# Scores as 64x64 tiles, two units in one train: a change to a fused attention and bilinear kernel on Trainium2

## The chip, the cores and the metric

The kernel runs on one core of one Trainium2 chip. The metric is the device time in microseconds (us), from one launch to its end; lower is better. "A unit" below is a block of 128 positions of one batch element, all eight heads. There are 4 x 6 = 24 of them.

## What is computed

A decaying linear attention in blocks, and behind it a bilinear feed-forward layer:

```
B, H, S, D = 4, 8, 768, 64
Dmask   = where(i >= j, lam ** (i - j), 0)              # inside a block
intra   = ((q_b @ k_b.T) * Dmask) @ v_b                 # scores, then attention output
inter   = (q_b * lam ** (i + 1)) @ kv_state             # what came before the block
out_b   = intra + inter
kv_state = lam ** block * kv_state + (k_b * lam ** (block - 1 - i)).T @ v_b

x = out.transpose(0, 2, 1, 3).reshape(B * S, H * D)     # 3072 x 512
y = ((x @ w_a) * (x @ w_b)) @ w_out                     # d_ff = 1536
```

The kernel takes blocks of 128 positions and puts the decay into scaled q and k.

## The kernel before

The 24 units are worked through in groups of 4, 2, 4, 4, 4, 4, 2. While TensorE does the feed-forward layer of one group, the attention of later units is put in between at "slots", by a plan. From group 1 on the products of the feed-forward layer are made with seven partial products in place of eight (`m_q`, `m_r`, `m_p` for the first two matrices, `o_q`, `o_p`, `o_r` for the last one); the additions this takes fall to VectorE and GpSimd.

The plan for groups 2, 3 and 4 ends with these steps; `_u` is 10, 14 and 18:

```python
for _g, _u in ((2, 10), (3, 14), (4, 18)):
    PLAN[_g] += [(11, "V", _u), (13, "Q", (_u, _u + 1, _u + 2)), (14, "V", _u + 2), (14, "S", _u + 3),
                 (16, "SK", _u + 4), (16, "OD", (_u + 2, _u + 3)), (17, "SM", _u + 4)]
```

V updates the state of a unit, S makes scores and masks them, SK makes scores and holds their banks, SM masks what SK left, Q makes the attention output of two units with the scores of a third, OD makes the output of two units.

PSUM has seven banks that rotate (an eighth holds the state). A bank is given out by longest-unused among those that are not held; reading a tile out, or releasing it, marks it as just used:

```python
    def ps_bank(name, shape, dt, hold=False, at=None):
        i = at
        if i is None:
            i = min((i for i in range(7) if i not in bank["held"]), key=lambda i: bank["age"][i])
        touch(i)
        if hold:
            bank["held"].add(i)
        ...
```

Scores, the products with the state (`inter`) and the attention products (`intra`). Where an operand or a result takes only 64 of the 128 partitions, the matmul uses only that half of the array's rows or columns:

```python
    def scores(u, kq=None):
        d = U[u]
        kq = kq or score_banks()                 # two banks, kq0 and kq1
        for hp in range(HP):                     # HP = 4 pairs of heads
            for i in range(2):
                p = slice(64 * i, 64 * i + 64)
                nc.tensor.matmul(kq[i][:, hp, :], lhsT=d["kT"][p, hp, :], rhs=d["qT"][p, hp, :],
                                 start=True, stop=True, skip_group_check=True)
        return kq

    def o_mm(u, b, c, **ops):
        h = 4 * b + c
        p = slice(64 * (h % 2), 64 * (h % 2) + 64)
        ...
        nc.tensor.matmul(U[u]["o"][b][p, c // 2, :], start=new[b, h % 2], stop=True, ...)

    def inter(u):
        if u % NB > 0:                           # NB = 6 units of a batch element
            st = st_bufs[(u - 1) % 4]
            for c in range(HP):
                for b in range(2):
                    p = slice(64 * b, 64 * b + 64)
                    o_mm(u, b, c, lhsT=st[p, c, b, :], rhs=U[u]["qT"][p, c, :])

    def intra(u, b):
        for c in range(HP):
            o_mm(u, b, c, lhsT=vbs[u][:, 4 * b + c, :], rhs=U[u]["m"](b, c))

    def pieces_O(us, nxt=(), defer=False):       # "Q": us = two units, nxt = the third
        kqs = [score_banks() for u in nxt]
        o_banks(us)                              # two banks o_ps for both units
        for u, kq in zip(nxt, kqs):
            scores(u, kq)
        for u in us:
            inter(u)
        for b in range(2):
            for u in us:
                intra(u, b)
            evac_o(us, b)                        # ScalarE copies o_ps[b] to xT, marks the bank
        ...
        if beside:
            kv_beside(us[1])                     # state products, 128x64
        ...                                      # masks of nxt, on VectorE; mark kq0, kq1

    def piece_SK(u):
        kq = U[u]["kq"] = scores(u)
        return kq.ids                            # the plan holds these two banks

    def piece_SM(u):
        kq = U[u].pop("kq")
        masks(u, kq)
        return kq.ids                            # the plan lets them go
```

The last matrix of groups 2 to 4, up to where o_r is taken (FC is 12):

```python
        q, qb = bank_of("o_q")                   # held
        product(q, of_x(0, 0), of_w(0, 0), js, True)
        s1 = snap("o_s1", "c12", q, 2)
        ...
            p, pb = bank_of("o_p")
            product(p, of_x(0, 1), of_w(1, 0), js[:2], True)
            xs4 = [blocks(j) for j in js]
            add_sums(js[:2], (0, 1))
            last_step()                          # last m_q product; VectorE: ab = c22 * m_q; m_q's bank released
            hook(FC)
            product(p, of_x(0, 1), of_w(1, 0), js[2:], False)
        o1, o2 = out_tile(), out_tile()
        nc.vector.tensor_add(o1[:, :, 0:256], s1, p)
        release(pb)                              # o_p's bank
        if not early:
            add_sums(js[2:], (0, 1))
        hook(FC + 1)                             # slot 13
        r, rb = bank_of("o_r")
        product(r, of_s(0), of_t(0), js, True)
        s5 = snap("o_s5", "s5", r, 2)
        if not early:
            hook(FC + 2)                         # slot 14
        ...
        product(q, of_s(1), of_t(1), js, False)
        u2 = snap("o_u2", "c12", q, 2)
        ...
        hook(FC + 3)
        hook(FC + 4)                             # slot 16
        product(q, of_s(2), of_t(2), js, False)
```

Of the kernel before, what the change touches and what calls it, by code (L numbers as in the profile page):

```python
# [61 lines left out]
    5: [(6, "SA", 23), (8, "SB", 23), (11, "V", 22), (13, "O2", (22, 23))],  # L62
}
for _g, _u in ((2, 10), (3, 14), (4, 18)):
    PLAN[_g] += [(11, "V", _u), (13, "Q", (_u, _u + 1, _u + 2)), (14, "V", _u + 2), (14, "S", _u + 3),
                 (16, "SK", _u + 4), (16, "OD", (_u + 2, _u + 3)), (17, "SM", _u + 4)]
PLAN[2] += [(_s, "W", None) for _s in (3, 3, 3, 4, 4, 4)]

# [2 lines left out]
def kernel(  # L71
# [11 lines left out]
    nc = tc.nc  # L83
    B, H, S, D = q.shape
# [244 lines left out]
    def score_banks():  # L329
        kq = Banks()  # L330
        kq.ids = []
        for i in range(2):
            kq.append(ps_bank(f"kq{i}", [128, HP, 128], F32))
            kq.ids.append(bank["last"])
# [4 lines that stand above are left out]
        kq = kq or score_banks()  # L339
        for hp in range(HP):  # L340
            for i in range(2):
                p = slice(64 * i, 64 * i + 64)
                nc.tensor.matmul(kq[i][:, hp, :], lhsT=d["kT"][p, hp, :], rhs=d["qT"][p, hp, :],  # L343
                                 start=True, stop=True, skip_group_check=True)
        return kq

    def masks(u, kq):
# [98 lines left out]
    def piece_S(u):  # L446
        masks(u, scores(u))

    def piece_SA(u):
        kq = U[u]["kq"] = scores(u)  # L450
        U[u]["ms"] = [mask_one(kq, 0)]
        return [kq.ids[1]]

    def piece_SK(u):
        kq = U[u]["kq"] = scores(u)
        return kq.ids
# [644 lines left out]
```

## Time and profile before

| what | value |
|---|---|
| time, median of 3 runs | 216.6 us (216.32 to 216.92) |
| span of the profiled execution | 214.6 us |
| TensorE clock granted | 1.00 |
| PE time by the chain, line 594 (m_q, m_r, m_p) | 25%, 13% and 6% |
| PE time by the chain, scores (kq, line 343) | 3% |
| score matmuls of units 4 to 23 (line 343) | 160, of 64 rows x 128 columns |
| state products into o_ps from these units (line 379) | 136 records, 64x64 |
| attention products into o_ps (line 379) | 192, of 128 rows x 64 columns |
| DMA, mean | 146 GB/s |

PE is TensorE's matmuls and PEld its weight loads; DVE is VectorE, ACT ScalarE, POOL GpSimd. A shape such as 64*128 behind a matmul is the part of the array used: rows by columns. A matmul's length in the profile runs to its modelled end and overlaps its neighbours', so the pace is read from one start to the next. Slots have no name in the profile; they are found by the order of tensors on PE.

### The profile page before, as it was taken

The numbers are of one execution on the slowest core, as the hardware profiler recorded it, in microseconds if no ns is written. First come the engines' busy times: TensorE is split into PE (matmuls) and PEld (weight loads), VectorE is DVE, ScalarE is ACT, GpSimd is POOL, SyncE is SP. The second block draws the span as 40 slices with busy tenths as digits, with TensorE's granted clock in tenths as the row PEclk, the third lists the DMA queues.
The fourth block names the chain that finished last, engine by engine and source line by source line (L and its number), as shares of the span: only waits on it lengthen the run. The fifth ranks groups of instructions, "written<-read, shape, count | busy, mean of one in ns | idle before, by whom it ended". The sixth has DMA issues, their size and how long they took to land.

```text
span 214.6 us, 5764 instructions
## 1 busy us (share of the span) xinstructions
PE 208.5 (97%) x2323; PEld 162.6 (76%) x2331; DVE 176.9 (82%) x322; ACT 106.8 (50%) x195; POOL 124.2 (58%) x143
## 2 busy tenths in 40 slices
PE   7899999999999999999999999999999999999994
PEld 2476444555995788878888988888988888889973
DVE  0892899987897997998989998989998788896860
ACT  3686224156852556436555534555444656343621
POOL 5879669983769299810699610799700846400320
PEclk9999999999999999999999999999999999999999
DMA  4999999999999999992299990399900480002202
GB/s 126 303 180 189 201 231 216 239 219 185 128 203 165 163 181 267 245 187 44 105 164 209 261 148 3 111 179 170 233 0 3 120 152 0 3 2 92 107 3 98
DMA packets 86766, 31.31 MB, mean 146 GB/s; under 512 B 74068, under 2 KB 83156, under 8 KB 86740
## 3 DMA queue, kind: packets, MB, share of 16 engines
q1 hardware_dynamic: 53748, 20.39, 48.0%
q0 software_dynamic: 32704, 10.49, 42.7%
q8 instruction: 18, 0.29, 0.6%
q10 hardware_dynamic: 288, 0.07, 0.1%
q14 instruction: 8, 0.07, 0.1%
HBM read 28.32 MB, written 6.29 MB: 161 GB/s over the span
## 4 chain that ended last, share of the span: by engine, by line
PE 93%; DMA 3%; SPq 1%; issue 0%; ACT 0%; DVE 0%
PE m_q L594 25%; PE m_r L594 13%; PE op L832 10%; PE o_q L705 9%; PE m_p L594 6%; PE o_r L705 5%; PE o_ps L379 5%; PE b_ps L517 5%; PE a_ps L517 5%; PE kq L343 3%; DMA k<-in_k_dram 3%; PE o_p L705 2%; PE kvd L410 2%; SPq L229 1%; PE tps L321 1%; PE o_w L705 1%
## 5 line engine op out<-in xcount | busy, mean ns | idle before, releaser
L594 PEld LDWEIGHTS <-tw 128*128 128x128 bf16 x576 | 48.7, 98 | 5.4
L641 POOL TENSOR_TENSOR ab<-c,c 128x512 bf16<-128x512 bf16 x30 | 34.9, 1170 | 28.2 <-DVE c L639 27.8
L594 PE MATMUL m_q<-xs,tw 128*128 128x256 bf16 (+1 forms) x288 | 36.1, 255 | 0.0
L594 PEld LDWEIGHTS <-wa_sb 128*128 128x128 bf16 x288 | 24.7, 98 | 2.6
L609 ACT COPY s<-m_q 128x512 f32<-128x512 f32 x30 | 17.7, 589 | 17.2 <-PE m_q L594 17.1
L648 DVE TENSOR_TENSOR ab<-c,m_q 128x512 bf16<-128x512 f32 x30 | 20.5, 684 | 5.9 <-PE m_q L594 4.0
L360 DVE TENSOR_TENSOR m<-kq,lotri 128x512 bf16<-128x512 f32 x39 | 24.6, 681 | 0.7 <-PE kq L343 0.7
L298 POOL DMA_DIRECT2D vb<-in_v_dram x24 | 22.4, 935 | 1.4 <-DMA wo_sb<-in_moe_w_out_dram 1.2
L832 PE MATMUL op<-wo_sb,ab 128*128 128x512 bf16 (+2 forms) x114 | 22.1, 335 | 0.4 <-issue 0.2
L639 DVE TENSOR_TENSOR c<-u,m_r 128x512 f32<-128x512 f32 x30 | 20.4, 681 | 2.3 <-ACT u L609 2.3
L609 ACT COPY s<-m_r 128x512 f32<-128x512 f32 x30 | 17.7, 590 | 9.0 <-PE m_r L594 9.0
L609 ACT COPY u<-m_q 128x512 f32<-128x512 f32 x30 | 17.7, 591 | 6.9 <-PE m_q L594 5.7
L645 DVE TENSOR_TENSOR c<-s,m_q 128x512 f32<-128x512 f32 x30 | 20.6, 686 | 0.6
L628 DVE TENSOR_TENSOR c<-s,m_p 128x512 bf16<-128x512 f32 x25 | 17.1, 686 | 3.9 <-PE m_p L594 3.6
L1039 POOL COPY gate<-xs 1x1 bf16<-1x1 bf16 x3 | 0.5, 178 | 34.3 <-DVE xs L575 34.3
L705 PEld LDWEIGHTS <-sm 128*128 128x128 bf16 x192 | 17.9, 98 | 2.9 <-DVE sm L738 0.2
L276 POOL TENSOR_TENSOR qk<-qf,lp_q 128x512 bf16<-128x512 f32 x18 | 18.9, 1048 | 0.0
L402 ACT CAST xT<-o_ps 128x512 bf16<-128x512 f32 x22 | 11.9, 589 | 13.4 <-PE o_ps L379 13.2
L594 PE MATMUL m_r<-xs,tw 128*128 128x256 bf16 (+1 forms) x144 | 18.1, 255 | 0.0
L594 PE MATMUL m_q<-xT,tw 128*128 128x256 bf16 (+1 forms) x144 | 18.1, 255 | 0.0
L594 PE MATMUL m_r<-xs,wb_sb 128*128 128x256 bf16 (+1 forms) x144 | 18.1, 255 | 0.0
L594 PE MATMUL m_p<-xT,wa_sb 128*128 128x256 bf16 (+1 forms) x144 | 18.1, 255 | 0.0
(120 smaller groups left out, 382.7 us busy)
## 6 DMA issues: line engine op xcount, KB each, us to landing
out_dram<-o_two SPq DMA_DIRECT2D x8, 512.0 KB, 3.2
qf<-in_q_dram SPq DMA_DIRECT2D x14, 256.0 KB, 5.4
kf<-in_k_dram SPq DMA_DIRECT2D x14, 256.0 KB, 5.8
vb<-in_v_dram POOLq DMA_DIRECT2D x24, 128.0 KB, 5.6
wa_sb<-in_moe_w_a_dram POOLq DMA_DIRECT2D x6, 256.0 KB, 6.2
wb_sb<-in_moe_w_b_dram POOLq DMA_DIRECT2D x6, 256.0 KB, 7.6
wo_sb<-in_moe_w_out_dram POOLq DMA_DIRECT2D x6, 256.0 KB, 8.1
out_dram<-o_kept SPq DMA_DIRECT2D x6, 256.0 KB, 5.1
```

Source lines behind the costliest of these rows:

```text
L276: eng_of(eng).tensor_mul(dst.rearrange("p (c b) d -> p b c d", b=2), x[:].rearrange("p (b c) d -> p b c d", b=2), lp.rearrange("p (b c) o ...
L298: nc.gpsimd.dma_start(out=vb, in_=vr[b, nb])
L360: nc.vector.tensor_mul(m, kq[i], lotri_bc)
L517: nc.tensor.matmul(ps[:, lo:hi], lhsT=w_sb[:, s, f * 128:(f + 1) * 128], rhs=xT[:, s, lo:hi], start=(s == 0), stop=(s == KS - 1), skip_gro ...
L594: nc.tensor.matmul(ps[:, f, :], lhsT=w(k, f), rhs=x[:, k, :], start=(first and f == 0 and k == 0), stop=True, skip_group_check=True)
L609: nc.scalar.copy(t, ps)
L639: nc.vector.tensor_add(c12, d["u2"], d["r"])
L641: nc.gpsimd.tensor_mul(ab[:, nf * i:nf * i + nf, 0:h], d["c11"], c12)
L645: nc.vector.tensor_add(d["c22"], d["s5"], d["q"])
L648: nc.vector.tensor_mul(ab[:, nf * i:nf * i + nf, h:2 * h], d["c22"], d["q"])
L705: nc.tensor.matmul(ps[:, t, :], lhsT=x(j, c)[:, t * BLK:(t + 1) * BLK], rhs=w(j)[:, c, :], start=(first and t == 0 and j == js[0] and c == ...
L832: nc.tensor.matmul(op[:, lo:hi], lhsT=ab[:, f, t * 128:(t + 1) * 128], rhs=wo_sb[:, f, lo:hi], start=(f == 0), stop=(f == FC - 1))
```

## The change

The scores of a unit are cut along the columns too: 16 matmuls of 64x64 in place of 8 of 64x128, the same shape that the state products have. Between a train of scores and the state products behind it TensorE then keeps its shape. In groups 2 to 4 the scores of unit `_u + 3` leave slot 14 and go ahead of those of unit `_u + 2` at slot 13, in one train with them, with their two banks held until slot 14, where VectorE masks them as before. Both parts are meant to spare TensorE changes of shape. On VectorE, ScalarE, GpSimd and the queues the order of instructions stays as it was; the banks that the tiles get are others.

```diff
 for _g, _u in ((2, 10), (3, 14), (4, 18)):
-    PLAN[_g] += [(11, "V", _u), (13, "Q", (_u, _u + 1, _u + 2)), (14, "V", _u + 2), (14, "S", _u + 3),
+    PLAN[_g] += [(11, "V", _u), (13, "SK", _u + 3), (13, "Q", (_u, _u + 1, _u + 2)), (14, "V", _u + 2), (14, "SM", _u + 3),
                  (16, "SK", _u + 4), (16, "OD", (_u + 2, _u + 3)), (17, "SM", _u + 4)]

@@ scores
         for hp in range(HP):
             for i in range(2):
                 p = slice(64 * i, 64 * i + 64)
-                nc.tensor.matmul(kq[i][:, hp, :], lhsT=d["kT"][p, hp, :], rhs=d["qT"][p, hp, :],
-                                 start=True, stop=True, skip_group_check=True)
+                for c in (0, 64):
+                    nc.tensor.matmul(kq[i][c:c + 64, hp, :], lhsT=d["kT"][p, hp, c:c + 64], rhs=d["qT"][p, hp, :],
+                                     start=True, stop=True, skip_group_check=True)
         return kq
```

## The prediction

> **What bounds the kernel now.** I read the page's table of engines first, then the chain that ended last. Columns of the first: busy time, share of the span, instructions.
>
> ```profile
> PE 208.5 (97%) x2323; PEld 162.6 (76%) x2331; DVE 176.9 (82%) x322; ACT 106.8 (50%) x195; POOL 124.2 (58%) x143
> ...
> PE 93%; DMA 3%; SPq 1%; issue 0%; ACT 0%; DVE 0%
> ```
>
> TensorE works from end to end, and the chain names no other engine after the first inputs have landed. The list of waits has only a few tenths of a microsecond for PE after the start. So every nanosecond put on or taken off the PE queue counts in full, and whatever makes PE wait is new time. Busy time does not show the tile mode, though: matmuls overlap, and a switch of mode hides inside a "busy" stretch. For that I read the time line of PE alone (start, length, engine, line, tensors, count), here at slot 13 of group 2:
>
> ```profile
> 93.32 0.60 PE L705 MATMUL o_p<-wo_sb,ab 128*128 128x256 bf16 x4
> 93.86 0.40 PE L343 MATMUL kq<-qkT 64*128 64x128 bf16 x8
> 94.18 0.42 PE L379 MATMUL o_ps<-qkT,st 64*64 64x128 bf16 x16
> 94.53 0.64 PE L379 MATMUL o_ps<-m,vb 128*64 128x128 bf16 x16
> 95.10 0.61 PE L705 MATMUL o_r<-two,sm 128*128 128x256 bf16 x4
> ```
>
> and from slot 14 to the end of slot 16:
>
> ```profile
> 96.56 0.39 PE L410 MATMUL kvd<-vb,qk 128*128 128x128 bf16 x4
> 96.88 0.40 PE L343 MATMUL kq<-qkT 64*128 64x128 bf16 x8
> 97.21 1.48 PE L705 MATMUL o_q<-two,sm 128*128 128x256 bf16 x12
> 98.63 0.40 PE L343 MATMUL kq<-qkT 64*128 64x128 bf16 x8
> 98.95 0.31 PE L379 MATMUL o_ps<-qkT,st 64*64 64x128 bf16 x8
> 99.19 0.64 PE L379 MATMUL o_ps<-m,vb 128*64 128x128 bf16 x16
> ```
>
> Read the differences of starts. Full-array matmuls of 256 columns follow each other every 0.109 us, so the four o_p should hand over at 93.32 + 0.44 = 93.76; the scores start at 93.86. That 0.10 us is the switch 128x128 to 64x128. A score train lasts 0.327 us from its first start to the next mode's first start (the single starts in the trace: 93.855 and 94.183). A train of 16 state products lasts 0.347 (94.183 to 94.530), one of 8 lasts 0.236 (98.952 to 99.188): 8 more cost 0.111, so four square tiles go through together every 0.056 us. The scores in pairs also have 0.056 us per pair.
>
> **What the Trainium skill says.** "TensorEngine Tiling (Array Packing)", Key Properties: changing the tiling mode drains TensorE, and different tiles load and multiply in parallel. The trace agrees with both: 0.09 to 0.10 us more at every change of shape, four square tiles per 0.056 us. The same page, Restrictions and Gotchas, says that column tiling switches off the fast weight load. The trace shows loads of 103 to 110 ns for 64 columns against 92 to 96 for the scores' 128, but the state products keep their 0.056 all the same, so I charge nothing for it. "PSUM — Partial Sum Buffer", Terms (PSUM bank): TensorE and a reader may not be on one bank at once. So a bank has to be read out before it is written again; no run here shows a collision, only waits.
>
> **The change part by part.**
> Square tiles. A unit's 8 score matmuls of 64x128 become 16 of 64x64: four rounds of four tiles in place of four pairs, at the same 0.056 us. Where full-array work stands on both sides the new train should look like the 16 state products: 0.347 against 0.327, +0.02 us. There are 160/8 = 20 trains. Ten stand alone (units 4 to 7, 9, 10, 11, 15, 19, 23): +0.20 us.
> Where state products come next there is no switch any more: 8 rounds in one mode cost 0.347 + 4 x 0.056 = 0.57 against 0.327 + 0.347 = 0.67, so -0.10 us. That is four trains without counting slot 13: unit 8 in group 1 and units 14, 18, 22 at slot 16: -0.41 us.
> The moved train. At slot 14 kvd's four matmuls should take 4 x 0.056 = 0.22 us, yet o_q starts 0.65 us after them. Without unit 13's scores there, 0.43 to 0.44 us go (the first matmul behind a switch is also 0.01 late). Three groups: -1.31 us. At slot 13 the four more rounds cost 0.22 us, less 0.10 for the switch saved: +0.12 each, +0.37 in all.
> Without new waits this sums to 0.20 - 0.41 - 1.31 + 0.37 = -1.15 us, 215.4 us. That is what the change is after.
>
> **Banks.** Slot 13 is where I think this fails. The seven rotating PSUM banks go out by longest-unused. o_q holds one. Before, the slot asks for two score banks and two for o_ps, and six are free: the two most recent, those of the last m_q and of o_p, stay untouched. Then o_r takes m_q's. Changed, the two banks of unit u+3 are held as well: 1 + 2 + 2 + 2 = 7. The two o_ps, asked for last, get exactly m_q's and o_p's banks. Both are still being read by VectorE:
>
> ```profile
> 94.01 0.68 DVE L648 TENSOR_TENSOR ab<-c,m_q 128x512 bf16<-128x512 f32 x1
> 94.61 0.68 DVE L771 TENSOR_TENSOR o_two<-o_s,o_p 128x512 f32<-128x512 f32 x1
> ```
>
> The order of instructions of the changed kernel has a wait for VectorE on the first matmul into each o_ps, which confirms it. VectorE works without a gap there, in an unchanged order, so it cannot come sooner. The first state product goes into m_q's bank; the second goes into o_p's and can start at 94.608 + 0.678 + 0.055 = 95.34 (0.055: after the sums of L738 end at 95.620, o_r goes on at 95.677). Two units' scores end at about 93.86 + 0.08 + 7 x 0.056 = 94.33, so PE stands for 1.0 us. Compared with 94.19 before, the second state product is 1.15 late.
>
> Then o_r. Four unheld banks are left, and the longest unused is o_ps's first, marked when ScalarE copies it out; the score banks are marked later, with the masks. The changed order has a ScalarE wait on the first o_r. The copy:
>
> ```profile
> 94.99 1.07 ACT L402 CAST xT<-o_ps 128x512 bf16<-128x512 f32 x2 [2.13 <-PE o_ps L379]
> ```
>
> The first of the two starts 0.456 after the attention products do (94.986 - 94.530) and takes 0.586; with 0.055 for the release, o_r may start 1.10 us after the attention products. Before, it starts 0.57 after them. That is 0.53 us more, of which 0.13 was spent later anyway on o_r's wait for its sums (four o_r from 95.10 end at 95.54, the fifth starts at 95.677).
> Group 2: 1.15 + 0.53 - 0.13 = +1.55 at the end of o_r; -0.44 for the moved train, -0.10 at slot 16: **+1.01 us**.
> Groups 3 and 4 have the same banks; VectorE is earlier in proportion:
>
> ```profile
> 125.93 0.42 PE L379 MATMUL o_ps<-qkT,st 64*64 64x128 bf16 x16
> ...
> 125.89 0.67 DVE L771 TENSOR_TENSOR o_two<-o_s,o_p 128x512 f32<-128x512 f32 x1
> ...
> 157.65 0.31 PE L379 MATMUL o_ps<-qkT,st 64*64 64x128 bf16 x8
> ...
> 157.61 0.67 DVE L771 TENSOR_TENSOR o_two<-o_s,o_p 128x512 f32<-128x512 f32 x1
> ```
>
> In group 3 the second state product can start at 125.887 + 0.674 + 0.055 = 126.62 against 125.93: +0.68. There eight kvd products lie between the attention products and o_r (0.69 instead of 0.57), so o_r waits 0.40 more. 0.68 + 0.40 - 0.44 - 0.10 = **+0.54**. Group 4: 157.612 + 0.729 = 158.34 against 157.65, the same sum: **+0.55**. These already contain the scores' 0.22, hidden in the stall.
> Sum: 1.01 + 0.54 + 0.55 + 0.20 (trains alone) - 0.10 (unit 8) = **+2.2 us**. 216.6 becomes 218.8; I take 218.7, as VectorE may catch up a little while PE stands.
>
> **Rivals.** (1) The gain comes as meant: 215.4. For it: each switch's 0.10 us is real and PE is the only bound. Against it: two named waits, on banks whose readers end after PE wants them. (2) Only the first wait bites, because the copies out of o_ps come sooner or o_r finds its bank free: 0.53 - 0.13 + 0.40 + 0.40 = 1.2 less, 217.6. Against it: ScalarE cannot start before the attention products it copies. (3) Square tiles are slower than state products, through 16 loads where 8 were, say 0.1 us a train: 20 x 0.1 = 2 more, 220.8. Against it: the state products, with the same shapes, show 0.056 per four. (4) Unit u+3's transposed q and k come too late at slot 13, some 3 us sooner than before. Against it: unit 13's transpose is issued at 82.1, 17's at 115.1, 21's at 148.7, and landing takes at most 7.5 us.
>
> **Range and chances.** The stalls are differences of measured ends and depend on one engine's fixed order; I give each 0.3 us. 217.5 to 219.7 holds most of it, down to rival 2 and up to half of rival 3. The 2% bounds are 212.3 and 220.9: faster would need over 4 us from switches that cost 0.1 each; slower needs rival 3 in full. Faster 0.01, within 0.96, slower 0.03.
>
> **What would show it.** PE's list of waits after the start should hold o_ps waiting for L771 three times (about 1.0, 0.5, 0.5 us as the trace sees idleness, less what running matmuls cover), and o_r for the copy of L402 three times, each about 0.4 to 0.5. Score trains next to state products without the 0.09 gap would show the first part right; score rounds slower than 0.056, or 0.35 us exceeded by a lone train, would show it wrong. If o_ps starts at once behind the scores, my reading of the banks is wrong, and the time goes to 215.4.

## The result, and the profile after

The changed kernel takes 218.68 us (median of 5 runs, 218.56 to 218.92) against 216.73 of the kernel before: 1.0088 times as long, 95% interval 1.0068 to 1.0109. It is slower by about 1.9 us (1.5 to 2.4 by the interval), inside the predicted 217.5 to 219.7. The profiled span is 217.1 against 214.6.

The page and the list of what TensorE (PE) waited for, in the changed kernel (engine, line, tensor, then the releaser; us in total, times, longest):

```profile
PE 207.9 (96%) x2491; PEld 163.1 (75%) x2491; DVE 176.1 (81%) x322; ACT 106.8 (49%) x195; POOL 124.7 (57%) x143
...
PE 85%; DVE 6%; DMA 3%; issue 1%; SPq 1%; ACT 1%
...
PE o_r L706 <- ACT xT L403: 1.1, 3, 0.5
PE o_ps L380 <- DVE o_two L772: 1.0, 3, 0.4
```

The kernel before had neither wait. PE falls from 93% to 85% of the chain that ended last, and VectorE (DVE) comes in with 6%: the chain now runs through the readers of PSUM banks, and from them back along VectorE's own work, so the 6% (13 us) are more than the stalls. On the time line of PE, slot 13 of group 2 (start, length, engine, line, tensors, count, idle time before and its releaser):

```profile
93.68 0.60 PE L706 MATMUL o_p<-wo_sb,ab 128*128 128x256 bf16 x4
94.21 0.64 PE L344 MATMUL kq<-qkT 64*64 64x128 bf16 x32
95.08 0.21 PE L380 MATMUL o_ps<-qkT,st 64*64 64x128 bf16 x1 [0.23 <-DVE ab L649]
95.68 0.41 PE L380 MATMUL o_ps<-qkT,st 64*64 64x128 bf16 x15 [0.39 <-DVE o_two L772]
96.02 0.64 PE L380 MATMUL o_ps<-m,vb 128*64 128x128 bf16 x16
97.12 1.47 PE L706 MATMUL o_r<-two,sm 128*128 128x256 bf16 x12 [0.46 <-ACT xT L403]
```

One state product starts, the other fifteen come 0.60 us later, and o_r stands once more. The idle times in brackets are shorter than the stalls, because a matmul's recorded length runs on after the next could have started: the starts say more. On VectorE and ScalarE (ACT) at the same place:

```profile
94.35 0.68 DVE L649 TENSOR_TENSOR ab<-c,m_q 128x512 bf16<-128x512 f32 x1
94.95 0.68 DVE L772 TENSOR_TENSOR o_two<-o_s,o_p 128x512 f32<-128x512 f32 x1
...
96.48 1.07 ACT L403 CAST xT<-o_ps 128x512 bf16<-128x512 f32 x2 [3.27 <-PE o_ps L380]
```

L649 ends at 95.03, and the first product starts at 95.08; L772 ends at 95.63, the others start at 95.68; the first copy ends at 97.07 and o_r starts at 97.12. Each time about 0.05 us after the end of the bank's reader.

Two measures serve for every run below, both in us and from the starts on PE in its profiled execution. The time from the first score of slot 13 to the first score of slot 16 holds nearly everything that the moved train touches. "Whole PE" is the time from the first score of group 0 to the last matmul. Neither has the noise of a launch (the first two profiles differ by 0.24 us before group 0's scores alone).

| kernel | group 2 | group 3 | group 4 | whole PE | device time against before, 95% interval |
|---|---|---|---|---|---|
| before | 4.771 | 4.755 | 4.643 | 200.31 | 1 |
| changed | 5.839 | 5.392 | 5.274 | 202.50 | 1.0088 (1.0068 to 1.0109) |
| e1, square tiles only | 4.780 | 4.667 | 4.557 | 200.00 | 0.9973 (0.9959 to 0.9987) |
| e2, moved train only | 5.867 | 5.386 | 5.277 | 202.68 | 1.0099 (1.0076 to 1.0123) |
| e3, square tiles beside state products only | 4.783 | 4.648 | 4.547 | 200.01 | 0.9976 (0.9960 to 0.9992) |
| e4, banks swapped | 6.062 | 5.606 | 5.496 | 203.17 | 1.0116 (1.0086 to 1.0147) |
| e5, copy in two halves | 5.910 | 5.451 | 5.340 | 202.70 | 1.0082 (1.0059 to 1.0105) |
| e6, o_p copied by ScalarE | 5.249 | 5.116 | 5.005 | 201.38 | 1.0032 (1.0018 to 1.0046) |
| e7, two banks fewer | 4.322 | 4.435 | 4.324 | 199.08 | 0.9933 (0.9917 to 0.9949) |
| e8, banks freed sooner | 4.608 | 4.730 | 4.618 | 199.95 | 0.9970 (0.9955 to 0.9986) |
| e9, as e3 | 4.770 | 4.647 | 4.541 | 199.85 | 0.9985 (0.9969 to 1.0001) |

### The profile page after: what moved, and what is told of

Its sections match the earlier page's. It is cut to its first block, busy times and chain, and to the rows that moved or that the text cites. A ratio compares the mean times of both kernels' runs of the same rounds, so it can differ in the third digit from the quotient of the medians.

```text
span 217.1 us, 6092 instructions
## 1 busy us (share of the span) xinstructions
PE 207.9 (96%) x2491; PEld 163.1 (75%) x2491; DVE 176.1 (81%) x322; ACT 106.8 (49%) x195; POOL 124.7 (57%) x143
## 4 chain that ended last, share of the span: by engine, by line
PE 85%; DVE 6%; DMA 3%; issue 1%; SPq 1%; ACT 1%
PE m_q L595 23%; PE m_r L595 12%; PE op L833 10%; PE o_q L706 7%; PE m_p L595 6%; PE o_r L706 5%; PE a_ps L518 5%; PE b_ps L518 5%; PE o_ps L380 5%; DMA k<-in_k_dram 3%; PE kq L344 2%; DVE sm L739 1%; SPq L229 1%; PE kvd L411 1%; DVE ab L649 1%
## 5 line engine op out<-in xcount | busy, mean ns | idle before, releaser
L649 DVE TENSOR_TENSOR ab<-c,m_q 128x512 bf16<-128x512 f32 x30 | 20.6, 685 | 5.9 <-PE m_q L595 4.0
L833 PE MATMUL op<-wo_sb,ab 128*128 128x512 bf16 (+2 forms) x120 | 23.1, 337 | 0.0
L595 PE MATMUL m_q<-xT,wa_sb 128*128 128x256 bf16 (+1 forms) x144 | 18.1, 255 | 0.0
```

Source lines behind the costliest of these rows:

```text
L595: nc.tensor.matmul(ps[:, f, :], lhsT=w(k, f), rhs=x[:, k, :], start=(first and f == 0 and k == 0), stop=True, skip_group_check=True)
L649: nc.vector.tensor_mul(ab[:, nf * i:nf * i + nf, h:2 * h], d["c22"], d["q"])
L833: nc.tensor.matmul(op[:, lo:hi], lhsT=ab[:, f, t * 128:(t + 1) * 128], rhs=wo_sb[:, f, lo:hi], start=(f == 0), stop=(f == FC - 1))
```

## The experiments

The theory: the two-unit train takes the last two free PSUM banks while VectorE still reads them, and o_r then has to take one that ScalarE still reads. The rivals: square tiles are slow; or the state products and o_r wait for something of their own.

### The two parts apart

**e1**, the plan of before and square tiles everywhere; **e2**, the other way round:

```diff
 # e1: before.py with
+                for c in (0, 64):
+                    nc.tensor.matmul(kq[i][c:c + 64, hp, :], lhsT=d["kT"][p, hp, c:c + 64], rhs=d["qT"][p, hp, :], ...)
 # e2: before.py with
+    (13, "SK", _u + 3), (13, "Q", (_u, _u + 1, _u + 2)), (14, "V", _u + 2), (14, "SM", _u + 3),
```

> Square score tiles with the plan of before. My theory (a switch of mode costs about 0.10 us, four square tiles go every 0.056 us, a lone square train costs 0.02 us more): 7 trains next to state products save 0.10 each, 13 lone ones lose 0.02 each, -0.46 us, 216.2 against 216.7 of before, no wait of PE on o_ps or o_r. Rival (square tiles are slower through 16 weight loads where 8 were, and this is what cost the 2 us): 217.5 or more.

> The two-unit train at slot 13 with the scores still 64x128. My theory (both stalls come from the two banks held more): the stalls are set by the end of VectorE's and ScalarE's reads, so they stay; groups 2 to 4 lose 1.11, 0.64 and 0.65, 219.1 us. Rival (the moved train by itself saves, and the loss comes from the square tiles): below 216.7.

e1 took 216.23 us against 216.69 of before, 0.9973 times; e2 took 218.78, 1.0099 times. The moved train alone costs what the whole change costs, and square tiles alone save a little. e2's median lies 0.3 us under the expected 219.1; on PE it is 2.37 us longer than before, where 2.40 was expected. In e2 the waits are those of the changed kernel:

```profile
93.90 0.62 PE L343 MATMUL kq<-qkT 64*128 64x128 bf16 x16
94.80 0.21 PE L379 MATMUL o_ps<-qkT,st 64*64 64x128 bf16 x1 [0.28 <-DVE ab L648]
95.40 0.41 PE L379 MATMUL o_ps<-qkT,st 64*64 64x128 bf16 x15 [0.39 <-DVE o_two L771]
95.74 0.64 PE L379 MATMUL o_ps<-m,vb 128*64 128x128 bf16 x16
96.83 0.38 PE L705 MATMUL o_r<-two,sm 128*128 128x256 bf16 x2 [0.46 <-ACT xT L402]
```

At slot 13 it makes no difference which shape the scores have: the switch that square tiles save is hidden in the stall.

e1's median came out as expected (-0.46), but that is luck: its interval is -0.9 to -0.3, and from the first score of group 0 to the last matmul it saves 0.31. Each of the seven trains beside state products was to save 0.10. In groups 3 and 4 and at slot 16 of group 2 they do: 0.248 us from the first score to the first state product in place of 0.327, and 0.024 more inside the state products. Two give nothing. In group 1, behind unit 8's scores, the state products of before and of e1, with VectorE's read of m_p:

```profile
61.18 0.69 DVE L628 TENSOR_TENSOR c<-s,m_p 128x512 bf16<-128x512 f32 x1 [0.28 <-PE m_p L594]
...
61.45 0.40 PE L343 MATMUL kq<-qkT 64*128 64x128 bf16 x8
...
61.78 0.45 PE L379 MATMUL o_ps<-qkT,st 64*64 64x128 bf16 x8
...
62.16 0.64 PE L379 MATMUL o_ps<-m,vb 128*64 128x128 bf16 x16
```

```profile
61.34 0.69 DVE L629 TENSOR_TENSOR c<-s,m_p 128x512 bf16<-128x512 f32 x1 [0.28 <-PE m_p L595]
...
61.60 0.42 PE L344 MATMUL kq<-qkT 64*64 64x128 bf16 x16
...
61.85 0.53 PE L380 MATMUL o_ps<-qkT,st 64*64 64x128 bf16 x8
...
62.31 0.64 PE L380 MATMUL o_ps<-m,vb 128*64 128x128 bf16 x16
```

From the first score to the attention products it is 0.70 us in both: the eight state products contain a pause that was 0.144 us before and is 0.224 now. VectorE's read of m_p ended last there already. It ends at 61.871 before and at 62.021 in e1; the second state product, the first into the other o_ps bank, starts at 61.924 and at 62.076, each time 0.05 us later, as at slot 13 of the changed kernel. The saved switch only lengthens that wait. That this o_ps has m_p's bank is inferred from these times; no run varied it. The second is slot 13 of group 2, where o_r waits for its third sum from VectorE: 1.62 us for its twelve matmuls before, 1.72 in e1. So five trains save 0.10, not seven, and 13 x 0.02 comes off again. Counted from the matmul ahead of a train to the one behind it, a train beside state products saves 0.106 and a lone one costs 0.018, so the terms make 5 x -0.106 + 13 x 0.018 = -0.30, which is what the profile shows (200.00 against 200.31).

**e3** makes only the trains that have state products behind them square, and **e9** is the same kernel once more:

```diff
+BESIDE_STATE = (8, 12, 14, 16, 18, 20, 22)
...
+                if u in BESIDE_STATE:
+                    # two 64x64 matmuls, as in the change
+                    continue
```

> Plan of before; square tiles only in the seven trains that have state products behind them (units 8, 12, 14, 16, 18, 20, 22), 64x128 in the thirteen lone ones. My theory: 7 x -0.10 = -0.7 us, 216.0. Rival (a switch costs the drain once per train whatever comes next): 216.7.

> The square tiles beside state products alone, once more on the same chip as the version with the banks freed sooner, as the best version without a moved train: 216.0 to 216.3 by the theory.

216.29 (0.9976) and 216.08 us (0.9985, interval 0.9969 to 1.0001, which reaches the kernel before). The expected -0.7 did not come: the same two trains save nothing, which leaves -0.5. Against e1 the clock tells no difference, although the lone trains are as they were expected to be: 0.350 us square and 0.330 not, from the first score to the next full-array matmul. Thirteen times 0.02 is 0.26 us, and the intervals reach 0.3 us or more to each side. On PE e9 saves 0.46 us and e3 0.31, because e3 has one more gap of 0.20 us in group 2 (76.11 to 76.42): VectorE (L651) reads m_q until 76.37, and the next product is added into the same bank 0.055 us later. In e9 PE loses 0.07 us at this place; why VectorE is later there than in the kernel before stays open.

### Is the wait that of a bank?

**e4** leaves the work of the changed kernel and asks for the banks in another order, so that the scores of unit u+2 get those of m_q and o_p:

```diff
-        kqs = [score_banks() for u in nxt]
-        o_banks(us)
+        if nxt:
+            o_banks(us)
+            kqs = [score_banks() for u in nxt]
...
```

> The changed kernel, but at slot 13 the two o_ps banks are asked for ahead of the scores of the third unit, so that these scores get the banks of m_q and o_p. My theory (the wait belongs to the bank, not to the state products): PE waits for L648's and L771's counterparts at kq in place of o_ps, ends that wait at the same time, and has 0.22 us more work left behind it, three times: +0.66 on the changed kernel's 218.7, 219.3. Rival (the state products wait for something of their own, such as the copied state): the wait stays at o_ps and the time at 218.7.

219.38 us, 1.0116 times. The wait has moved with the bank:

```profile
94.25 0.42 PE L344 MATMUL kq<-qkT 64*64 64x128 bf16 x16
95.12 0.24 PE L344 MATMUL kq<-qkT 64*64 64x128 bf16 x2 [0.46 <-DVE ab L653]
95.72 0.41 PE L344 MATMUL kq<-qkT 64*64 64x128 bf16 x14 [0.35 <-DVE o_two L776]
95.92 0.44 PE L380 MATMUL o_ps<-qkT,st 64*64 64x128 bf16 x16
```

The state products, which now have banks that are free, start without a pause. The three groups are longer than the changed kernel's by 0.223, 0.214 and 0.222 us, where 0.22 was expected: the work that used to come ahead of the wait now comes behind it.

**e6** gives o_p's bank back sooner. ScalarE, idle there, copies o_p out, and VectorE adds from the copy:

```diff
-        nc.vector.tensor_add(o1[:, :, 0:256], s1, p)
...
+        else:
+            p_out = sn_pool.tile([128, nt, 256], F32, name="o_po", tag="u2", bufs=1)
+            nc.scalar.copy(p_out, p)
+            nc.vector.tensor_add(o1[:, :, 0:256], s1, p_out)
         release(pb)
```

> The changed kernel with o_p first copied out of PSUM by ScalarE, which is idle there; VectorE then adds from the copy, so o_p's bank comes free earlier. My theory: the second state product can start at 94.74 in place of 95.34 in group 2 (then m_q's reader ends last) and at about 0.26 earlier in groups 3 and 4; -1.1 us on 218.7, 217.6, with the waits of o_r unchanged. Rival (what frees the bank late is VectorE's order as a whole, or ScalarE's copies of o_ps are pushed back by as much): 218.5 to 218.9.

217.65 us, 1.0032 times; the groups are shorter by 0.59, 0.28 and 0.27, where 0.60, 0.26 and 0.26 were expected. In group 2 all sixteen products now wait for m_q's reader and for nothing else; o_r waits as before:

```profile
94.29 0.64 PE L344 MATMUL kq<-qkT 64*64 64x128 bf16 x32
95.16 0.42 PE L380 MATMUL o_ps<-qkT,st 64*64 64x128 bf16 x16 [0.23 <-DVE ab L649]
95.51 0.64 PE L380 MATMUL o_ps<-m,vb 128*64 128x128 bf16 x16
96.60 1.47 PE L706 MATMUL o_r<-two,sm 128*128 128x256 bf16 x12 [0.46 <-ACT xT L403]
```

**e5** lengthens what o_r waits for: the copy of the first o_ps bank in two instructions.

```diff
+        if eng == "act" and b == 0 and us[0] in (10, 14, 18):
+            for h in range(2):
+                nc.scalar.copy(dst[:, h], ...)          # 128x256 each
```

> The changed kernel with ScalarE's copy of the first o_ps bank at slot 13 of groups 2 to 4 cut into two instructions of 128x256, which take about 0.39 + 0.37 in place of 0.59 us. My theory (o_r waits for this copy because it gets its bank): o_r starts 0.17 us later three times, +0.5 on 218.7, 219.2. Rival (o_r waits for the sums of VectorE, or the copy is hidden): 218.7.

218.9 us: against the changed kernel too close to tell by the clock, and the expected +0.5 did not come (whole PE is 0.20 longer). The profile says why: my estimate of the two copies was wrong, not the wait. The two halves take 0.372 and 0.378 us, but start 0.268 apart, so both are done after 0.65 us, not 0.76:

```profile
96.43 0.65 ACT L404 CAST xT<-o_ps 128x256 bf16<-128x256 f32 x2 [3.28 <-PE o_ps L380]
```

This is 0.06 more than the 0.586 of the whole copy, and from the attention products to o_r it is 1.154 us in place of 1.093: 0.061 more (0.683 against 0.622 from the kvd products in group 3). o_r follows the end of this copy.

### Is the order of the work good, without the bank pressure?

**e7** keeps all instructions of the changed kernel but takes two banks fewer at slot 13: the scores of unit u+2 are written over those of unit u+3, and both masks read the same banks. It leaves out that unit u+3 has scores of its own, so it is a measure of time and no version to use.

```diff
-        kqs = [score_banks() for u in nxt]
+        kqs = [U[u + 1]["kq"] if u in (12, 16, 20) else score_banks() for u in nxt]
```

> The changed kernel with all its work, but at slot 13 the scores of unit u+2 are written over those of unit u+3, into the same two banks, and both masks read these. It leaves out that unit u+3 keeps scores of its own (they are overwritten), and so takes two banks fewer at slot 13. My theory (the order of TensorE's work is good, only the seventh and sixth bank cost time): no wait on o_ps or o_r beyond those of before, 216.7 - 1.15 = 215.5 us. Rival (the train of two units hurts for another reason as well, such as later masks or transposes): 216.7 or more.

215.25 us, 0.9933 times. Same matmuls, same masks, no stall:

```profile
94.18 0.64 PE L344 MATMUL kq<-qkT 64*64 64x128 bf16 x32
94.65 0.39 PE L380 MATMUL o_ps<-qkT,st 64*64 64x128 bf16 x16
94.97 0.64 PE L380 MATMUL o_ps<-m,vb 128*64 128x128 bf16 x16
95.54 1.50 PE L706 MATMUL o_r<-two,sm 128*128 128x256 bf16 x12
```

So the change's idea is worth about 1.5 us by the clock (1.1 to 1.8) and 1.2 on PE (199.08 against 200.31), and two banks turn it into a loss of 1.9.

**e8** tries to get there with every result kept: e6's copy; in group 2 the sums that are needed late go behind the product that frees m_q's bank; VectorE masks the first score bank of unit u+2 at once, with the late sums and the addition of o_p behind it, and o_r takes that bank.

```diff
             scores(u, kq)
+            U[u]["ms"] = [mask_one(kq, 0)]
+            bank["free"] = kq.ids[0]
+            bank["put_off"][0]()
...
-            add_sums(js[:2], (0, 1))
+            lead = (0,) if u0 == 6 else (0, 1)
+            add_sums(js[:2], lead)
             last_step()
...
+            p_out = snap("o_po", "u2", p, 1)
+            release(pb)
...
+            r, rb = bank_of("o_r", bank["free"])
```

> The changed kernel, all results kept, with the three readers brought forward: ScalarE copies o_p out; in group 2 VectorE makes the product that frees m_q's bank ahead of two sums that are needed later; VectorE masks the first score bank of unit u+2 directly behind, and o_r takes this bank in place of o_ps's. My theory: at most 0.1 us is left of each stall, and the two-unit train then brings what it was meant to: 216.7 - 1.15 = 215.5 us (as in the run that overwrote the scores, 215.25). Rival (VectorE has no room for this order, and TensorE waits for the sums or masks put back): 216.5 or more.

216.15 us against 216.58, 0.9970 times (0.9955 to 0.9986). That is faster than the kernel before and the changed one, but 0.6 us short of what I expected, and no better than square tiles alone: e9, timed against the same runs of the kernel before, took 216.08. o_r no longer stands; the state products still do:

```profile
94.59 0.64 PE L344 MATMUL kq<-qkT 64*64 64x128 bf16 x32
...
94.69 0.59 ACT L730 COPY o_po<-o_p 128x512 f32<-128x512 f32 x1 [1.10 <-PE o_p L712]
...
95.06 0.69 PE L380 MATMUL o_ps<-qkT,st 64*64 64x128 bf16 x16
...
95.68 0.64 PE L380 MATMUL o_ps<-m,vb 128*64 128x128 bf16 x16
96.25 1.49 PE L712 MATMUL o_r<-two,sm 128*128 128x256 bf16 x12
```

From their first start to the attention products it is 0.62 us in place of 0.324 (in group 4, with eight products, 0.51 in place of 0.21): in all three groups the second product starts 0.27 us after the first. It waits for o_p's bank, which ScalarE's copy frees about 0.9 us after the last o_p begins (0.27 for the matmul, 0.59 for the copy; it ends at 95.28, and the second product starts at 95.33), while the first state product is due after 0.67. My estimate for e6, only 0.26 sooner in groups 3 and 4, had this remainder in it; here I forgot it. The three groups are 0.29 us longer than e7's each, which is all that e8 lacks against it (216.15 - 215.25 = 0.9).

## Why the prediction was right

**The stalls at o_ps.** Predicted: the second state product at 95.34 in group 2, 126.62 in group 3, 158.34 in group 4, in the time of the kernel before. Taking off the shift of the last o_p (94.008 - 93.650 in group 2, then 1.339 and 1.887), the trace has 95.32, 126.62 and 158.34. e2, e4 and e6 show that the bank is the cause and the readers' ends the size: with the moved train alone the stall stays, with the banks swapped it goes with the bank, and with an earlier reader it shrinks by as much.

**The stall at o_r.** Predicted 1.10 us from the attention products to o_r; measured 1.093. e5 moves it by exactly as much as the copy is longer, and e8, where o_r has another bank, removes it.

**The sums of the groups.** From slot 13 to slot 16, +1.11, +0.64 and +0.65 were predicted (the group's sums without the 0.10 saved behind slot 16's scores) and +1.07, +0.64 and +0.63 measured.

**Square tiles.** A lone train costs 0.02 more, as predicted. The 16 loads of 64 columns cost nothing: rounds of four follow every 0.056 us, as the state products did. Scores and state products in one mode save 0.10, at slot 16 three times as predicted. The step that failed is unit 8's -0.10: nothing came of it, because the wait for VectorE's read of m_p, which the kernel before has too (a pause of 0.144 us), grew by as much. At 0.1 us it does not show in the total.

**The rivals.** "The gain comes as meant", 215.4, is what e7 shows to lie behind the two waits (215.25; on PE -1.23 us, where the prediction's sum without waits is -1.15). "Only the first wait bites" fell with o_r's 1.1 us in the list of waits, "square tiles are slower" with e1, "the transposes come too late" with e7, which has no wait at all at slot 13.

**The total.** The sum was +2.2 us, of which I took 0.1 off because VectorE might catch up while PE stands. Measured is +1.95, by the interval 1.5 to 2.4, which cannot tell these apart. No run shows VectorE catching up: the stalls have the predicted size without it, and on PE the changed kernel is 2.19 us longer (202.50 against 200.31), the sum itself. That the median of 218.68 falls beside the 218.7 is luck.

## What to carry to other kernels

Before work is moved earlier, count the PSUM banks held at that point and name the last reader of each bank that the allocator will hand out: in a longest-unused rotation the marginal requests get exactly the banks that were freed in the program last, whose readers are still running, and the tile that waits may be an innocent one two steps later (o_r here). A saving on the critical engine counts only where nothing else ends just behind it: of seven saved mode switches two went into waits for VectorE that were already there, though neither stands in the list of PE's waits before. Test such a theory by moving the wait (another bank order) and by a run with the same instructions and fewer buffers; the two together separate the worth of the idea from the price of its buffers.

## What the runs showed of the hardware that was not expected

Two ScalarE copies of 128x256 from PSUM behind one another start 0.268 us apart though each is recorded with 0.372 to 0.378 us, so cutting a copy of 0.586 us in two costs only 0.06 us. The Trainium skill has this ("ScalarE: Activation LUTs", What ACT_TABLE_LOAD costs: back-to-back ACTIVATE instructions overlap by about 93 ns); for these copies the trace shows 104 ns, which is what counts here, and my estimate for e5 added lengths instead. A square score train costs 0.350 us between full-array matmuls and an oblong one 0.330, for the same number of multiplications. The 0.02 was predicted; most of it is in the first round, 0.080 us to the second against 0.067, and the rest in the last, where four starts take 0.010 us and two 0.003.
